# Attention in another order, slot sums copied in halves, and the last part's start resequenced

## Chip, core and metric

The kernel runs on one core of one Trainium2 chip. The metric is device microseconds (us) of one execution. TensorE (PE, with its weight loads PEld) multiplies, VectorE (DVE), ScalarE (ACT) and GpSimd (POOL) work elementwise, and SyncE (SP) issues most of the DMAs. Products go into PSUM, which has eight banks of 512 float32 columns; the other operands lie in SBUF.

## The reference

Three layers, one behind the other, all in float32: attention with pooled queries, a soft mixture of eight experts with four slots each, and a feed-forward layer with g = h cos h.

```python
q_pool = q.reshape(B, H, S // 2, 2, D).mean(axis=3)      # (4, 8, 576, 64)
attn = softmax(scale * q_pool @ k^T)                     # keys: 1152
x = (attn @ v) -> (2304, 512)
logits = x @ phi                                         # 32 slots
d = softmax(logits, over tokens); slot_in = d.T @ x
slot_out[e] = relu(slot_in[e] @ w1[e]) @ w2[e]
c = softmax(logits, over slots);  x2 = c @ slot_out
h = x2 @ w_in; g = h * cos(h); out = g @ w_out           # (512, 2048), (2048, 512)
```

## The kernel before

The kernel has two parts. The first holds attention and the mixture of experts. Its `attention()` only makes a list of 2,677 small operations, each a function with its dependencies; a string, `ORDER`, gives the sequence in which they are emitted (two characters of `DIGITS` are the number of one operation), and `in_order` walks it. So the order on every engine's queue is what `ORDER` says. An operation that needs a place takes the next free one: `"2"` are four places of two PSUM banks each, `"E"` five places in SBUF for exponentials, `"W"` twenty for expert weights. A place comes free when the last operation that uses its content has been emitted, and its next taker waits on the chip until that one is done.

Two heads are one pair `p`, 16 pairs in all; the queries of a pair are worked in two halves `a`, the 1152 keys in nine blocks `t`. For a pair, `sum_q` adds pooled neighbours (VectorE), `tr_q` and `tr_k` transpose (TensorE), `q_hi`, `k_hi` round to the fast format on ScalarE and `q_lo`, `k_lo` keep the rest on VectorE. `max_pair` multiplies rounded parts for a first maximum, `max_pair_red` reduces it on VectorE, `max_neg`, `max_row` and `max_put` turn it into a row. `scores(p,a,t)` is eight matmuls, `exps` the exponential on ScalarE, `av` the product with v, `av_out` its copy. `e_sum(p,a,t)` adds the exponentials up on GpSimd, or on VectorE where the digit t stands in `VEC[2*p+a]`. `load_v(p)` issues the DMA of v on SP's queue. Spread among this is `conv_*(i)`, which brings the last layer's weights to a rounded form for a fast product: loads, two passes on ScalarE, three on VectorE, `conv_round` on GpSimd, and `conv_store` back to DRAM on SP's queue.

At the end of the first part `o_mm` sums the slot outputs in one PSUM bank, `so_copy` (L1029) brings them to SBUF, `so_turn` (L1033) transposes and spreads them into four blocks of 128 columns, `so_put` (L1041) copies those to `soT`. `c_back(3)` and `c_keep(3)` do the same for the last token weights `cT`; in `ORDER` the sequence is so_copy, c_back(3), so_turn, so_put, c_keep(3).

The second part is emitted as the tuple `START` says, and then by a loop. `load_win_q` and `load_w` issue 1 MB DMAs of the converted weights. `p` (`p_some`, L1580) multiplies soT with 128 columns of w_in and keeps a rounded high part and a low part in `Pst`; `r` (`p_rows`, L1593) does it for 1,024 columns at once with 32 rows a piece, giving p_hi and p_lo, which `q` (`p_put`, L1609) spreads over Pst. A unit is one or two blocks of 128 columns of w_in for 256 tokens. `u` (`emit_u`, L1634) multiplies Pst and cT, ScalarE and VectorE bring the phase into range; `g` takes the sine and square on ScalarE, g, hi on VectorE and lo on GpSimd; `o` (`emit_o`, L1666) multiplies hi with w_hi and w_lo, and lo with w_hi. `s` (`split_w`, L1562) splits w_out's block f: a copy to w_hi by VectorE if `SPLIT[f]` is 2 or 3, otherwise by ScalarE, and the subtraction that leaves w_lo by GpSimd if it is odd, otherwise by VectorE. The first block of tokens has units of f = 0; 1; 2, 3; 4, 5; and so on. So o3 needs w of f = 4 and 5, o4 of 6 and 7, o8 of 14 and 15. The last unit's result is copied in halves by ScalarE and VectorE before its store (L1684).

Of the kernel before, what the change touches and what calls it, by code (L numbers as in the profile page):

```python
# [30 lines left out]
SPLIT = (0, 1, 1, 3, 1, 1, 1, 3, 2, 0, 1, 0, 3, 3, 0, 1)  # L31
# [23 lines left out]
    "1ZYJYL1O1S1P1T1X2V2W10112X1b1c2e2f1d4Q2c1W1a1e1g1h1k1l2d4SYM1o1i1s1p1tYN2k2lYKYO2-301f1j1m1n1r2Y1x2Z1y2i1q1u1v1w"  # L55
    "2g1-2j2hYQYP1z2031322324272o2p282m1+222n2q6T2t2u4V4W2xYR262AYS2y2B2r002s214Y4T25364U374X393D3AYTYU3E6W4Z4a3H3I4b"
    "296U3BYV2C3F3J3L2D2v2z383MYWYX2+2E3C3G3K3O3P2w4c4d3Q3R3U3V334g4h3Y3Z4e34354f3c2F4k3N3d2G4l3h3i3k4m4x3S3W3T4yYY2H"
    "2I3l3X4nYZYa3b3f3g4s4t3o3pYb3s3w3a3m3q4oYc4i3t3uYd3jYe3x3n3r3v3z4j3+4p3-Yg404q4r433eYf3y444u47484B55412J42454649"
    "4C2K56cAYh4A4E4F534R514v4w6X54526Y6b5A5D5B5H5LYjYk5E5FYl5P4-4D5I5J6Z5MYi5C5G5K5O8r506a6c5Q5S5N4z5TYo6d4+6e6fYmYn"
    "5U5V575Y5c5Z5d6u6v5g5h6k4G4H4I58595X6l5b5fYp6V5j5R5W8uAv5aYq73Yr5e5i5l5k5m745o5p8s5q5s5t6g5w5+Ys5x6h634JYt5-6q6r"  # L60
    "6i6j4K4L5n5r5vYuYv645u5y67686m6n6w6x5z61Yw714M62726B6F6C6G6o6s608x8yYx6p6t666A8v6y6z65696D8w6+8+6E8z6H6I6J4N8-90"
    "7E7H4O917F7I7J7L7P7MYzY+7Q6-7T707UcB6K6L92Y-Ay6M757776937G7KYy7O7S7W7XZ07896977N7R7V7Y7c7Z7g7d9E7h7k9F797A7b7f7B"
    "9A6N7l9I9J9BZ2Z17C7j7D7n7oZ3Z48t7p7a7e7q7s7t98Z56O6P7w7+7xAw7i99Z67u7y827-94959C9D6Q7r7v7zCz8180Z783858687889G8B"
    "ZA9H8C9K8F8G8J849NAz9L8K7mZ8Z9898D8H8A8E9O8I8M9McCA+B19TZB8N9c9d9U9f9gZD9j8L6R9k9P6S9QZCZE9n9o9h9l9r9pZF9sZG8O8P"
    "8QA-B3B09R9SZIcDB49e9i9mB2B59q9u9vBE9V9w9+BF9x9WZH9-8RA2A6A39X9YBA8S9t9y9zA7A1A59Z9aA0BB8T8U9bA9AAABAEA4A8D0ZJZK"
    "ACAFBGBHZLAIAJC+AMAQANZMAGB8ARBKAxZNZOBLADAHALB9APATAUBCBDAVAW8V8WAZAaAdAKAOB6ZQAhAeB7BIBJAi8X8YZP8ZBMBNASBVBWAY"
    "AcAgD1BOBPZRZTAkBQ8aAlD2D5ZSBgBhF1AXAbAfAjBjBnZUBkBZBlBoBaZVBrBvBsD3Bw8bBp8cD4BtB+ZYZWBTBiBUB-BmBqD6D7D8D9BXBYAm"
# [11 lines left out]
    "KSKMHMKTJPK8K9KEKWKbKXKfHNLkKQKUKJKNKRNhKVKZKcLlLmKYaZcNabKgKaKdKFKGHFHGHHHIcOacKjKhKkadagKnKoKsaaaeKvLxKeKiKmaf"  # L79
    "KtKwKxKlKpKqJQJRLyL-KrH9HAKzcPM0K+K-L1L2LrLsM1M2HOHQHPahL5LnJSajakNfHRLpaiL6alLoLqamKuJTKyL0L4L8L9LvLwLALzLBL+L3"  # L80
    "L7LELFLILJLtLuLMLNM3M6M7NkNlNnNiNjM4M5LCNmaoLDanaparLGLKLHLLLPLQMLMMMAMBMOMSMWMaasLOMPMQMTJUMXMEatQ3MbMNMRMVMUMZ"
    "MdMYMFMcMGJVM8aqawMeMfMjMHMgMnMkMrM9NtauMhMCMoMDavNuMiMlMmNgMIMqMsMuMvMpNoQ4NpNvMJMKNwNqaxLRLSayN-O0azMwMxMzN1Nr"
    "Q6MtM+N2N5N6N9NENsM-NAa+Nxa-O3LTN3N7b0MyNFO4N0NyN4N8NCNDNBNIO5NMNJNzO6b2NNNQN+O1NRLUO2O7cQQ9QAQCNGQDNHNLNPQELVLW"
# [1692 lines left out]
```

## Time and profile before

| | |
|---|---|
| runs | 731.6, 734.51, 735.19 us (median 734.51) |
| profiled execution | 732.33 us, span 730.5 us |
| TensorE busy | 717.4 us (98%) |
| VectorE, ScalarE, GpSimd busy | 569.7, 447.9, 407.2 us |
| attention and experts | to about 495 us of the span |
| head of the second part | 495 to 535 us |
| its steady part | 535 to 726 us |
| granted TensorE clock | 1.000 |

Busy time is the union of what the profiler shows of an engine's instructions. Matmuls overlap in the pipeline, so a short stop of TensorE is partly covered by the end of the matmul before it. A row of the timeline gives start, duration, engine, line, operation, and in brackets the idle time before it and what ended it.

### The profile page before, as it was taken

To read this page: it belongs to the slowest core of one execution; us is meant where nothing else is said; L and a number is where in the kernel's file an instruction comes from. 1 tells how busy PE (TensorE), PEld (TensorE's weight loads), DVE (VectorE), ACT (ScalarE), POOL (GpSimd) and SP (SyncE) were. 2 spreads that over 40 slices of the span, in tenths; PEclk is the share of its full clock that TensorE was granted. 3 is DMA by queue.
4 is the path that set the end of the run, shared out by engine and by line. 5 is a ranking of instruction groups with operands and counts; after the bars stand their busy time and mean duration, and the time that the engine had idled before them with its cause. 6 is when DMAs were issued, how large, how long until landed. Compare 5 with 4: busy or idle time off the path is not lost.

```text
span 730.5 us, 16465 instructions
## 1 busy us (share of the span) xinstructions
PE 717.4 (98%) x6428; PEld 530.7 (73%) x6428; DVE 569.7 (78%) x921; ACT 447.9 (61%) x846; POOL 407.2 (56%) x347
## 2 busy tenths in 40 slices
...
GB/s 221 145 98 157 173 134 130 209 162 141 191 130 187 199 156 160 182 191 102 171 102 147 183 163 259 360 410 414 11 30 30 0 30 30 30 9 20 31 29 30
DMA packets 75970, 101.48 MB, mean 139 GB/s; under 512 B 47156, under 2 KB 47540, under 8 KB 74996
## 3 DMA queue, kind: packets, MB, share of 16 engines
...
q14 instruction: 27, 0.22, 0.1%
...
## 4 chain that ended last, share of the span: by engine, by line
PE 89%; DVE 5%; DMA 2%; ACT 2%; issue 1%; POOL 0%; SPq 0%; DVEq 0%; ACTq 0%
PE mx L576 20%; PE o L1677 17%; PE mx L533 15%; PE o L1679 8%; PE mx L487 7%; PE mx L536 5%; PE u L1641 2%; PE mx L990 2%; PE mx L514 1%; PE mx L447 1%; PE mx L422 1%; DMA vn<-in_v_dram 1%; DMA w<-in_moe_w_dram 1%; PE mx L606 1%; DVE nm L496 1%; PE mx L384 1%
## 5 line engine op out<-in xcount | busy, mean ns | idle before, releaser
L565 POOL TENSOR_TENSOR ES<-ES,E 128x576 f32<-128x576 f32 (+2 forms) x149 | 215.5, 1447 | 93.0 <-DVE ES L565 54.9
L496 DVE TENSOR_REDUCE nm<-mx 128x2 f32<-128x768 f32 x240 | 220.8, 949 | 21.5 <-PE mx L487 20.3
L547 ACT ACTIVATE E<-mx 128x576 f32<-128x576 f32 (+2 forms) x288 | 175.1, 652 | 59.2 <-PE mx L536 42.3
L533 PE MATMUL mx<-Q,kX 64*128 64x288 f32 (+2 forms) x1152 | 163.8, 302 | 0.2 <-DVE avs L592 0.2
L576 PE MATMUL mx<-E,vn 128*64 128x288 f32 (+2 forms) x1152 | 157.8, 413 | 0.7 <-DMA vn<-in_v_dram 0.6
L1661 POOL TENSOR_TENSOR lo<-g,hi 128x512 fp32r<-128x512 f32 (+1 forms) x73 | 94.0, 1288 | 109.3 <-DVE hi L1659 103.1
L533 PEld LDWEIGHTS mx<-Q,kX 64*128 64x128 f32 x1152 | 109.6, 184 | 11.0 <-issue 2.6
L576 PEld LDWEIGHTS mx<-E,vn 128*64 128x64 f32 x1152 | 75.7, 136 | 57.0 <-ACT E L547 6.1
L1677 PE MATMUL o<-w_hi,hi 128*128 128x512 f32 x288 | 113.0, 392 | 0.6 <-DVE hi L1659 0.6
L1679 PE MATMUL o<-w_lo,hi 128*128 128x512 f32 x288 | 113.1, 393 | 0.3 <-DVE w_lo L1568 0.3
L533 PE MATMUL mx<-Q,kY 64*128 64x288 f32 (+2 forms) x576 | 87.4, 292 | 0.0
L536 PE MATMUL mx<-NM,one_row 64*128 64x288 f32 (+2 forms) x576 | 87.4, 291 | 0.0
L487 PE MATMUL mx<-kX,Q 64*128 64x384 f32 x490 | 84.7, 370 | 1.3 <-ACT Q L394 0.5
L1646 ACT ACTIVATE t<-u 128x512 f32<-128x512 f32 (+1 forms) x73 | 42.9, 591 | 58.6 <-PE u L1641 58.5
L1648 DVE SCALAR_TENSOR_TENSOR r<-t,u 128x512 f32<-128x512 f32 (+1 forms) x73 | 49.3, 678 | 36.3 <-ACT t L1646 35.7
L1677 PE MATMUL o<-w_hi,lo 128*128 128x512 f32 x288 | 77.3, 389 | 0.0
L1657 DVE SCALAR_TENSOR_TENSOR g<-r,u 128x512 f32<-128x512 f32 (+1 forms) x73 | 49.6, 679 | 35.2 <-ACT r L1655 34.4
L319 POOL TENSOR_TENSOR cvt<-cvt 128x512 uint32<-128x512 uint32 x32 | 40.9, 1279 | 46.4 <-ACT cvt L297 24.9
L487 PEld LDWEIGHTS mx<-kX,Q 64*128 64x128 f32 x490 | 44.1, 185 | 25.7 <-issue 10.9
L1677 PEld LDWEIGHTS o<-w_hi,lo 128*128 128x128 f32 x288 | 54.1, 188 | 11.3
L1677 PEld LDWEIGHTS o<-w_hi,hi 128*128 128x128 f32 x288 | 54.1, 188 | 10.8 <-DVE hi L1659 0.8
L1679 PEld LDWEIGHTS o<-w_lo,hi 128*128 128x128 f32 x288 | 54.2, 188 | 10.2 <-DVE w_lo L1568 0.6
...
## 6 DMA issues: line engine op xcount, KB each, us to landing
...
```

The costliest lines, as they stand in the source:

```text
L487: nc.tensor.matmul(out=m[:, h, 0:384], lhsT=Q1[p % 2][hs, AT[i]:AT[i] + 128], rhs=X[p][hs, ks], start=True, stop=True)
L496: nc.vector.tensor_reduce(out=nm3[p][:, i, :, c:c + 1], in_=m[:, :, 0:384], axis=AX.X, op=ALU.max)
L533: nc.tensor.matmul(out=sc[:, h, 0:n_q], lhsT=x[hs, ks], rhs=y[hs, qs], start=(n == 0), stop=False)
L536: nc.tensor.matmul(out=sc[:, h, 0:n_q], lhsT=one_row[hs, :], rhs=NM[p % 2][hs, qs], start=False, stop=True)
L547: nc.scalar.activation(out=e, in_=sc[:, :, 0:n_q], func=AF.Exp, scale=1.0 / 16.0)
L565: eng.tensor_tensor(out=ES[p, a], in0=ES[p, a], in1=E[p, a, t], op=ALU.add)
L576: nc.tensor.matmul(out=av_t[p, a, g][64 * h:64 * h + 64, 0:n_q], lhsT=vn[p][:, h, t, :], rhs=E[p, a, t][:, h, :], start=(t == g), stop=(t ...
L1648: nc.vector.scalar_tensor_tensor(out=r, in0=t, scalar=MAGIC, in1=u, op0=ALU.subtract, op1=ALU.subtract)
L1657: nc.vector.scalar_tensor_tensor(out=g, in0=r, scalar=1.0, in1=u, op0=ALU.subtract, op1=ALU.mult)
L1661: nc.gpsimd.tensor_tensor(out=lo[:, 0:n], in0=g, in1=hi[:, 0:n].bitcast(FP32), op=ALU.subtract)
L1677: nc.tensor.matmul(out=o, lhsT=x, rhs=w_hi[ff], start=(ff == 0 and not part), stop=bool(part and ff == NF - 1))
L1679: nc.tensor.matmul(out=o, lhsT=x, rhs=w_lo[ff], start=False, stop=False)
```

## The change

- `ORDER` is another sequence of the same operations in three stretches of attention: places 153 to 421 and 433 to 824 (about 32 to 76 and 76 to 153 us of the span) and 1494 to 1718 (269 to 309 us). Places 300 to 375, among them conv_store(3) at 323 and load_v(2) at 346, are the same.
- Seven strings of `VEC` differ; in all, VectorE has one `e_sum` fewer and GpSimd one more.
- `so_copy` copies in two halves on ScalarE, `so_turn` writes two PSUM banks instead of one, `so_put` copies the first half on ScalarE and the second on VectorE.
- The two `p` become one, `p_first`: both column blocks with the first half of the contraction, then both with the second. `r` for r = 0 is cut in three (quarter, quarter, half) with u0 and u1 between.
- Both `load_win_q` are issued ahead of both `load_w`.
- The splits come later, in the order of f; three copies and one subtraction go from VectorE to ScalarE and GpSimd. o2 is cut in two (8 products, then 4 by lo) with q(2,2), g4 and s6 between.
- The last result is copied by ScalarE alone.

```diff
-SPLIT = (0, 1, 1, 3, 1, 1, 1, 3, 2, 0, 1, 0, 3, 3, 0, 1)
+SPLIT = (0, 1, 1, 3, 1, 1, 1, 3, 1, 0, 1, 0, 1, 1, 0, 1)
 START = (
-    ("s", 1), ("p", 0, 0, 128), ("s", 2), ("p", 0, 128, 256), ("u", 0), ("s", 0), ("u", 1), ("g", 0),
-    ("r", 0), ("s", 3), ("g", 1), ("q", 0, 1), ("q", 1, 2), ("u", 2), ("o", 0), ("s", 5), ("s", 6), ("s", 4), ("u", 3),
-    ("g", 2), ("u", 4), ("o", 1), ("g", 3), ("r", 1), ("g", 4), ("s", 7), ("o", 2), ("q", 2, 2), ("s", 11), ("u", 5),
-    ("u", 6), ("s", 9), ("s", 10), ("q", 3, 2), ("s", 14), ("g", 5), ("o", 3), ("s", 8), ("s", 15), ("o", 4),
-    ("g", 6), ("s", 13), ("s", 12), ("u", 7), ("g", 7), ("u", 8), ("u", 9), ("o", 5), ("g", 8), ("u", 10),
+    ("p",), ("r", 0, 0, 1), ("u", 0), ("r", 0, 1, 2), ("u", 1), ("g", 0), ("r", 0, 2, 4), ("s", 0), ("q", 0, 1),
+    ("q", 1, 2), ("s", 1), ("g", 1), ("u", 2), ("o", 0), ("s", 2), ("s", 3), ("u", 3), ("u", 4), ("o", 1), ("s", 4),
+    ("g", 2), ("r", 1), ("s", 5), ("g", 3), ("o", 2, 0, 4), ("q", 2, 2), ("g", 4), ("s", 6), ("o", 2, 4, 8), ("s", 7),
+    ("u", 5), ("u", 6), ("s", 8), ("q", 3, 2), ("s", 9), ("g", 5), ("o", 3), ("s", 10), ("s", 11), ("o", 4),
+    ("g", 6), ("s", 12), ("s", 13), ("u", 7), ("g", 7), ("u", 8), ("u", 9), ("o", 5), ("s", 14), ("s", 15), ("g", 8), ("u", 10),
     ("g", 9), ("o", 6), ("u", 11), ("g", 10), ("o", 7), ("o", 8), ("o", 9),
 )
...
 VEC = (
-    "6", "1", "1268", "235", "1267", "26", "378", "13458",
-    "26", "18", "4", "38", "17", "56", "258", "1246",
-    "158", "3", "34567", "7", "125", "2", "36", "13456",
+    "6", "1", "178", "235", "1267", "27", "15", "1248",
+    "28", "138", "4", "38", "17", "56", "258", "1246",
+    "158", "3", "34567", "27", "125", "2", "36", "13456",
...
     def so_copy(i):
-        nc.scalar.activation(out=sh["so"], in_=sh["o"], func=AF.Copy)
+        for j in range(2):
+            cs = slice(j * DM // 2, (j + 1) * DM // 2)
+            nc.scalar.activation(out=sh["so"][:, cs], in_=sh["o"][:, cs], func=AF.Copy)
     def so_turn(i):
-        sh["s"] = mx()
+        sh["s"] = mx2()
...
-                out=sh["s"][:, kk * 128:(kk + 1) * 128], lhsT=sh["so"][:, kk * 128:(kk + 1) * 128],
+                out=sh["s"][:, kk // 2, kk % 2 * 128:(kk % 2 + 1) * 128], lhsT=sh["so"][:, kk * 128:(kk + 1) * 128],
...
     def so_put(i):
-        nc.vector.tensor_copy(out=sh["soT"].rearrange("p k s -> p (k s)"), in_=sh["s"])
+        for j in range(2):
+            o, x = sh["soT"][:, 2 * j:2 * j + 2].rearrange("p k s -> p (k s)"), sh["s"][:, j, 0:256]
+            if j:
+                nc.vector.tensor_copy(out=o, in_=x)
+            else:
+                nc.scalar.activation(out=o, in_=x, func=AF.Copy)
...
         for f in range(2):
             load_win_q(f)
+        for f in range(2):
             load_w(f, 2 - f)
...
-        def p_some(f, c0, c1, pm):
...
+        def p_first(pms):
+            for k0 in (0, 2):
+                for c, pm in enumerate(pms):
+                    cs = slice(128 * c, 128 * c + 128)
+                    for kk in range(k0, k0 + 2):
+                        nc.tensor.matmul(
+                            out=pm[:, 0:128], lhsT=soT[:, kk, :], rhs=win_q[0, kk][:, cs], start=(kk == 0), stop=(kk == HP - 1),
+                        )
+            for c, pm in enumerate(pms):
+                cs = slice(128 * c, 128 * c + 128)
+                nc.scalar.activation(out=Pst[0][:, cs], in_=pm[:, 0:128], func=AF.Copy, scale=INV2PI)
...
-        def p_rows(r, pm):
+        def p_rows(r, pm, k0=0, k1=HP):
             pm = pm[:, 0:256]
-            for kk in range(HP):
+            for kk in range(k0, k1):
...
+            if k1 < HP:
+                return
...
-                if last:
-                    h = DM // 2
-                    nc.scalar.activation(out=ob[:, 0:h], in_=o[:, 0:h], func=AF.Copy, scale=-TWOPI)
-                    nc.vector.tensor_scalar(out=ob[:, h:], in0=o[:, h:], scalar1=-TWOPI, scalar2=None, op0=ALU.mult)
-                else:
-                    nc.scalar.activation(out=ob, in_=o, func=AF.Copy, scale=-TWOPI)
+                nc.scalar.activation(out=ob, in_=o, func=AF.Copy, scale=-TWOPI)
...
-            for x in sorted(todo, key=lambda x: x[0]) if last else todo:
+            for x in (sorted(todo, key=lambda x: x[0]) if last else todo)[a:b]:
```

## Rows read from the trace of the kernel before

**Rows 1.** Windows: length, busy PE, PEld, DVE, ACT, POOL; clock, DMA share, GB/s

```profile
32.20:76.00 43.80, 42.58 (x454) 31.08 (x454) 42.56 (x60) 27.18 (x48) 28.87 (x22) 1.00 0.49 129
76.00:153.00 77.00, 77.00 (x889) 57.24 (x887) 71.83 (x110) 50.59 (x96) 51.78 (x41) 1.00 0.55 150
269.00:309.00 40.00, 40.00 (x439) 28.71 (x437) 36.60 (x54) 26.64 (x49) 26.60 (x21) 1.00 0.56 155
...
532.88:725.90 193.02, 192.99 (x902) 160.79 (x902) 115.01 (x192) 117.70 (x206) 84.48 (x65) 1.00 0.08 23
```

**Rows 2.** Timeline: the two matmuls that wait in the first stretch

```profile
48.16 0.45 PE L487 MATMUL mx<-kX,Q 64*128 64x384 f32 x2 [0.47 <-DVE kY L464]
...
74.23 1.16 PE L576 MATMUL mx<-E,vn 128*64 128x288 f32 x7 [0.65 <-DMA vn<-in_v_dram]
```

**Rows 3.** Waits of PE, 494 to 535 us: us in total, times, longest

```profile
PE pm L1583 <- DVE soT L1043: 0.8, 1, 0.8
PE u L1641 <- ACT Pst L1620: 0.7, 1, 0.7
PE pm L1614 <- ACT p_hi L1603: 0.6, 1, 0.6
PE o L1677 <- DVE hi L1659: 0.6, 2, 0.3
PE u L1641 <- DVE Pst L1589: 0.5, 1, 0.5
PE o L1679 <- DVE w_lo L1568: 0.3, 1, 0.3
PE u L1641 <- DVE g L1657: 0.2, 1, 0.2
```

**Rows 4.** Timeline: the first two products of o4

```profile
519.14 0.39 PE L1677 MATMUL o<-w_hi,hi 128*128 128x512 f32 x1
519.37 0.39 PE L1679 MATMUL o<-w_lo,hi 128*128 128x512 f32 x1
```

**Rows 5.** Groups by shape: running sums; busy us, mean ns, idle before

```profile
L565 POOL TENSOR_TENSOR ES<-ES,E 128x576 f32<-128x576 f32 x136 | 196.9, 1448 | 89.3 <-DVE ES L565 52.3 <-ACT E L547 10.2 <-DVE ES L563 7.7
L565 DVE TENSOR_TENSOR ES<-ES,E 128x576 f32<-128x576 f32 x73 | 55.6, 767 | 1.1 <-ACT E L547 0.2
```

**Rows 6.** Timeline: slot sums, from so_copy to the first product

```profile
495.84 0.60 ACT L1031 ACTIVATE so<-mx 128x512 f32<-128x512 f32 x1 [14.83 <-PE mx L1023]
...
496.49 1.16 PE L1036 MATMUL mx<-gsel,so 128*128 128x128 f32 x8
...
497.68 0.69 DVE L1043 COPY soT<-mx 128x512 f32<-128x512 f32 x1 [17.33 <-PE mx L1036]
...
498.43 2.05 PE L1583 MATMUL pm<-win_q,soT 128*128 128x128 f32 x16 [0.78 <-DVE soT L1043]
```

**Rows 7.** Timeline: the last result's two halves

```profile
725.95 0.38 ACT L1686 ACTIVATE ob<-o 128x256 f32<-128x256 f32 x1 [0.97 <-PE o L1677]
726.37 0.42 DVE L1687 TENSOR_SCALAR ob<-o 128x256 f32<-128x256 f32 x1 [0.93 <-ACT ob L1686]
```

**Rows 8.** Window of the first products, columns as in rows 1

```profile
498.43:503.42 4.99, 4.48 (x50) 3.16 (x50) 2.65 (x7) 2.98 (x8) 2.42 (x2) 1.00 1.01 422
```

**Rows 9.** Timeline: the row product and the first product of p_lo

```profile
501.49 1.93 PE L1599 MATMUL pm<-win_q,soT 128*32 128x256 f32 x32
...
504.41 0.39 PE L1615 MATMUL pm<-p_lo,spread 128*128 128x256 f32 x1
```

**Rows 10.** Timeline of POOL: a first split, a late one, a low half

```profile
498.31 1.26 POOL L1568 TENSOR_TENSOR w_lo<-w_lo,w_hi 128x512 fp32r<-128x512 f32 x1 [7.36 <-DMA w_lo<-w32o]
...
515.93 1.76 POOL L1568 TENSOR_TENSOR w_lo<-w_lo,w_hi 128x512 fp32r<-128x512 f32 x1
...
521.25 1.40 POOL L1661 TENSOR_TENSOR lo<-g,hi 128x512 fp32r<-128x512 f32 x1 [1.69 <-DVE hi L1659]
```

**Rows 11.** Groups by shape, POOL, 503 to 522 us: splits

```profile
L1568 POOL TENSOR_TENSOR w_lo<-w_lo,w_hi 128x512 fp32r<-128x512 f32 x6 | 8.3, 1396 | 0.8 <-ACT w_hi L1566 0.4 <-DVE w_hi L1564 0.4
```

More of the change, by code (lines that the diff above doesn't have):

```diff
@@ L54 @@
     "13151617191A1D1E0n1H0v1I2O2P0o0r2MYG142N182Q0w2R2S0s1B1F2T0l0m2U1C1G1K1L2a2b1MYH1Q1N0j1R0k1U0x1J1VYI1Y4P0t0y0u0-"
[L55 to L67, printed above, removed]
+    "1ZYJYL1O1S1P1T1X2V2W10112X1b1c2e2f1d4Q2c1W1a1e1g1h1k1l2d4SYM1o1i1s1p1tYN2k2lYKYO2-YQ1fYP1j1n1r302Y2Z1x1y2i1v1w2j"
@@ new lines @@
+    "2g2h1m1q1-203123322724281u2m2n1z212o2p2qYR1+222t2u4V2x2y262A2B4W2r4T4Y2s36393D4U4X6T373H3A3LYT3EYU253I6WYVYY292C"
+    "3M3B4Z2D2v2w2E3F2z2+4a336UYSYW383J3N3C3G3K3O344b3P35YX4g4h3Q3R4c4d3U3V3Y3Z4k4l3c3d4e4f3h3i3k3S3W2F2G4m4nYZYa4x4y"
+    "3T3X3b3f2H3l3m3a3g4s004tYb2I3o3s3w3p4o3qYc4i3t3uYd3jYe3x3n3r3v3z4j3+4p3-Yg404q4r433eYf3y444u47484B55412J42454649"
+    "4C2K56cAYh4A4E4F534R514v4w6X54526Y6b5A5D5B5H5LYjYk5E5FYl5P4-4D5I5J6Z5MYi5C5G5K8r6a6c5Q5O5N5S504z5TYo6d6e4+6fYmYn"
+    "5U5V575Y5c5Z5d6u6v5g5h6k6l4G4H4I58595X5bYpYq6V5R5W8u5f5jAv5a73Yr5e5i5l5k5m745o5p8s5s5t6g5w5+Ys5q636h4JYt5x5-6q6r"
@@ new lines @@
+    "6i4K5n5r6j5v5zYu6m644L4M6w5uYw5y60616n626x676o686p6B6C6F6G71726s6t8x8y8+6yYvYx8v658wYy8zcBYz696D666A6E6z6+6I6J8-"
+    "904N7E7H4O7L7F6H917P7T7I7M7Q7775Y+6K7U7G7K7O6L6MY-AyAw7J7N7679787A92Z0Z1937S7W7X6-707B7Y7Z7R7c967d977V7a7gZ27k9E"
+    "7e7h7i9A7b7f9F9B6N7j7l7n7o7C989IZ37D99Z47m7p7qCz9J7s7tZ57wZ6Z7ZA6O6P7u7x7+827y7-809C839D7r7v7z816Q85cC8694958788"
+    "9G9H8B9K8F8C848G8J8K9P9Q9T9UAz9L9M8A8E8I8MA+B1Z88NZ9898DZB9N9O9c9d9f9g8HZD8L9j9h8t9k9n9o6R9r6SZE9sZFZI9l9p8O8P8Q"
+    "A-B0B39tB49R9SZCZGB2ZH9e9i9m9qB59u9vBEBF9w9+9x9y9-9V9WA2A6A38R8S9X9Y9ZA7BG9zA18TA58U9a9bA0ZJA4A9BHAxD0AAABACBABB"
@@ L68 @@
+    "AEAFAIAJAMBKAQZLA8AGANAKB8B9BLZMZNADZKZOAHALAPARATAUBCBD8VAVcDAZAdAW8WAaAOASAeB6B7AhBIBJ8XZQAi8Y8ZZPZRZSBMBNBOAX"
+    "AbAf8aBVBWAYAcD1BPD2D5C+AgAkBQAlBgZTBhBjBnBkBZBrBvF1AjBoZUBaBsBwD38b8cZVBlBpD4B+BtZYZWBTBiBUB-BmBqD6D7D8D9BXBYAm"
     "BuAnAoByBxBz8d8eC-Bb8h8iC2C6C0BcBRC3CAC4F4C7C8CBZXZZZaBSDKBdDLC1C5C9CDCEcE8lCC8mcFBeBfHS8f8gDM8j8kDNCFCGCIZbZcCJ"
@@ L78 @@
     "J3J8JCJGJpJqLhLeLfLjLiH5H6J-HDKCKDHEJ9JDJHJLLcK0JKH7H8aRaTJMaUaVaSK1aWHJaXHKHLHBHCKAKHKBaYKKKIKLKOKPK4K2K5JNJOK3"
[L79 to L83, printed above, removed]
+    "KSKMHMKTJPK8K9KEKWKbKXKfHNLkKQKUKJKNKRNhKVKZKcLlLmKYaZcNabKgKaKdKFKGHFHGHHHIKjacKkNfKnKoKsKvLxcOKeaaKiKmKhKqadag"
+    "KtaeH9KlKpKwLyKxKrHAJQJRL-M0KzK+M1M2L1L5L2L6K-LrLsafahHOHQHPLpaiLnJSLvajHRakalJTKuKyaoL0L4LoLwL8L9amLqLALBLzL+LE"
+    "LFLILtLJLML3M6LuM3LNM7L7NkNlNnNiNjcPM4M5NmanaparLCLGLKLOLDLHLLLPLQNgaqMLMMMAMBMOMSMWMaMPasMTMQatMUMXMEJUMFMYauMN"
+    "MRMVMZMbMdJVMeMGawMfMHMgM8MjMnavMkM9MrNtMcMhMoNuMCMiMmMDMIMsMqMuMvNoQ3NvMJNpMKNwNqMlaxLRLSLTN-O0MwMxMzN1M+NrMpMt"
+    "azN2Q6N5N6NsN9NEa+M-N3N7NxO3NAayMya-N0N4O4N8NCNFNDNyO5O6NINJNMNNQ4Nzb2b0NBN+NQO1NRLUO2O7cQQ9QAQCNGQDNHNLNPQELVLW"
     "QFOCOEODO8LXO9NTb1NKNOS7NSOKOFb3b4OPNUOSOQb5OTOLOWOaOXOIObb6OeOJOGOHOfcRQ7ORQ8QBOVOZOALYb7QSOdOhOBLZNVOiNWOMONOO"
```

31 lines of the change are left out of this document (13 added, 18 removed).

## The prediction

> **What bounds the kernel now.** I read the busy shares by stage first, then the matmuls' waits, then the order of time where a wait stands. In the three stretches of attention whose order is rewritten TensorE is the bound: of 43.80 us it is busy 42.58, and in the other two for all of 77.00 and 40.00, at the full granted clock, while VectorE is busy 42.56, 71.83 and 36.60 [rows 1]. So a new order can win there only the 1.2 us in which no matmul runs. Two rows hold it: a max matmul at 48.16 waits 0.47 for VectorE's low half of k, a values product at 74.23 waits 0.65 for v [rows 2]. In the last part's head, 494 to 535, seven rows of waits add up to 3.7 us [rows 3]. A product of 512 columns is shown 0.39 long and is issued every 0.23 [rows 4], so a wait shown costs about 0.16 more than it says: eight waits, some 5 us in all. From there to the last product TensorE is busy 192.99 of 193.02 us [rows 1]. What can be won is thus some 1.5 us in attention, 5 in the head and a little at the end.
>
> **Attention.** The same operations are issued in another order, and seven strings of VEC differ, so that VectorE has one running sum fewer: 0.77 us off VectorE, 1.45 on GpSimd [rows 5]. Over the 161 us of the stretches that is nothing for either; it matters only where one of the two is late. The wait at 48.16 goes by the order: the matmul's PSUM bank came from k_lo(2,1) on VectorE, queued behind a conversion step and a sum of q; in the new order it comes from exps(1,0,4) on ScalarE, which has slack (27.18 busy of 43.80 [rows 1]). Worth 0.47 and the hidden 0.16: 0.6. The wait for v stays: load_v(2) keeps its place (346) in the order, behind the same conversion store on SP's queue, and a TensorE that comes earlier waits longer for it, unless the one VectorE sum less brings the conversion forward too. Count 0, bound 0.8. Against that, scores(1,0,3) now takes the bank of q_lo(2) with no TensorE work in between, where four other operations lay before; if VectorE is late there, it costs as much as a row of this kind, 0.5 to 0.8. Behind it are all the scores of that pair. Whether such places are worse in the other two stretches no row shows; their banks come as close before as after. I take 0.4 gained, with -1.2 (two new waits) and +1.5 as ends.
>
> **Slot sums.** Before: ScalarE copies so (495.84, 0.60), TensorE turns it (496.49, 1.16), VectorE copies soT (497.68, 0.69), and the first product starts at 498.43 [rows 6]. A half of 256 columns takes 0.38 on ScalarE and 0.42 on VectorE [rows 7]. After: the first half of so is there at 496.2, the turn can start about 496.3 (TensorE is at the weights' transposes until then), its first half is copied by ScalarE beside the turn of the second, and VectorE copies the second at 497.5. so_put stands ahead of c_keep(3) in ScalarE's queue, so the copy of cT, as large as so's (0.60 [rows 6]), is pushed behind it, to some 498.2; the first u needs it at 499.8, so this costs nothing, and would cost what it is late beyond 499.8 if that cover went. Then p starts at about 497.5: 0.9 earlier. Its second contraction half needs VectorE's half at 497.9 and comes to it at 498.4.
>
> **First rows and u.** Its sixteen matmuls took 2.05 with the drain of the last [rows 6]; the next can be issued from 499.4 on. The row product is cut in quarters and put between u0 and u1, so the wait of 0.5 for Pst [rows 3] is filled. It needs the second win_q block, moved ahead of w_lo on SP's queue; it lands some 2.5 us earlier than now, at 499.0 at the latest (1 MB at 422 GB/s [rows 8], counted back from the row product's start at 501.49 [rows 9]). The 32 row matmuls with u0 and u1 between them take 2.1, to 501.5, against 503.4 [rows 9]. p_hi now stands on ScalarE behind the sine and square of unit 0, p_lo on VectorE behind its g and hi; with four steps of 0.4 from u0's t, p_lo is there at 503.0, and its product follows at 503.05, against 504.41 [rows 9]: 1.4 kept. The wait for p_hi (0.6 [rows 3]) remains.
>
> **Splits.** The splits of f=1 and f=2 ran on GpSimd from 498.31 on, when it had nothing else [rows 10]. Now they stand behind the row product: ScalarE copies s0 after p_hi, then Pst's quarter, then s1, so GpSimd gets s1 at about 504.4. From there to w_lo7, which o4 needs, GpSimd has ten wide operations and a narrow one. Alone one takes 1.26, the worst took 1.76 [rows 10]; in the busy stretch the mean of a split is 1.40 [rows 11]. Ten at 1.40 and 0.75 is 14.7; and it idles about a microsecond before unit 4's low half, since that unit's sine waits on ScalarE for Pst2's copy, and that for q(2,2) behind the first eight products of o2. So w_lo7 is there at some 520.3 (519 to 521). After it o4 has seven of its twelve products left, 1.6 us: it ends at 521.9. Before it ran from 519.14 without a wait, twelve at 0.23, to 521.9 [rows 4]. The 1.4 us are spent at o4, to within 1 us. Then comes what VectorE is spared: the casts of f=8, 12 and 13 go to ScalarE and the subtraction of f=8 to GpSimd, 3 x 0.42 + 0.69 = 2 us by the nearest rows on VectorE [rows 6, 7]. Behind them stood the subtraction that o5 waits for (0.3), the g that frees u11's bank (0.2) and the hi that o8 waits for (half of 0.6) [rows 3]: 0.8 shown, 1.3 with what is hidden. GpSimd's seven wide operations from 520.3 to unit 7's low half take 9.8, to 530.1, which is just when o7 comes to it; s14 and s15 now stand ahead of g8, 1.2 us on ScalarE, which had waits to spare here. I take 1.2 for the whole head; ends -1 (GpSimd late by one more operation) and 3.6.
>
> A split on GpSimd took 1.26 at 498.31, in a quiet stretch, and 1.76 at 515.93, in a busy one [rows 10]. The Trainium skill (SBUF — State Buffer, Who interferes with whom) says that a VectorE instruction with two SBUF inputs and a GpSimd instruction that reads SBUF exclude each other, and the second waits for the first to end. By that rule every split moved from idle to busy time could pay what the 1.76 shows; by the mean of the rows it pays 0.14. The sum goes by the mean.
>
> **The last store.** Before, the two halves ran one after the other, ScalarE 725.95 and VectorE 726.37 to 726.79 [rows 7]. One copy of 512 columns is 0.60 [rows 6]: 726.55, 0.24 earlier, and nothing lies beside it.
>
> **Sum.** 0.4 + 1.2 + 0.24 = 1.8 us. The profiled execution took 732.33 with a span of 730.5; it would take 730.5. It lies 2.2 below the median of the runs, 734.51 (731.6 to 735.19), which becomes 732.7.
>
> **Rivals.** *All waits go:* GpSimd's operations cost 1.29 or less and its order leaves no gap, so that o4 keeps what the start won and the three later waits go too, 3.6; both waits of attention go, 1.2; with 0.24 that is 5.0 and 729.5. For it speaks that GpSimd idles for 1.69 until 521.25 before [rows 10]; against, that it must now do two splits more after 504. Chance 0.22. *Nothing is kept but the store:* the start's gain is spent at o4, the spared VectorE time is spent by s14, s15 and a late low half, and attention's new wait equals the one removed: 734.3. For it: what sets the end of a queue of eleven operations is its start, and that moves 6 us later. Chance 0.22. *Slower, by GpSimd and VectorE in each other's way:* at 1.76 for each wide operation w_lo7 comes at 523.0 and o4 ends at 524.6, and nine more to unit 8's low half end at 538.8, so that o8 ends 4.1 us later than now; less 0.24 and 0.4 that is 3.5 slower, 738.0. It decides from a mean of about 1.53 on; the mean of 1.40 before, with less crowding, is the evidence on both sides. At a mean of 1.65 it gives 736.3. Chance 0.10.
>
> **How the numbers follow.** The forecast, 732.7 (731 to 734), has 0.46. The range of 729.2 to 735.8 leaves out half of the first rival and more than half of the last. A measurement of this kernel can tell 0.5%, 3.7 us, from no change: faster means below 730.8, slower above 738.2. Faster: most of the first rival and the low edge of the forecast, 0.25. Slower: the top of the last and an attention with several new waits, 0.06. Within: 0.69.
>
> **What would show it.** Right: the first product of soT at 497.5 less what attention gained, relative to the last slot product; the row product ended 1.9 earlier; a wait of o4 for GpSimd's w_lo; no wait of o5, u11 and o8; 0.24 at the end; attention's rewritten stretches shorter by under 1 us. Wrong: a wide GpSimd operation in the head above 1.5 or below 1.3 on average; o4 without a wait; matmul waits of half a microsecond in attention that were not there.

## The result, and the profile after

The changed kernel takes 739.25 us (median of ten runs, 735.28 to 745.52), the kernel before 734.74 beside it (731.6 to 738.25). The ratio is 1.0071, 95% interval 1.0042 to 1.0100: slower by some 5 us, where 1.8 us faster were forecast, and with a spread of 10 us instead of 7. The profiled execution took 738.41 us with a span of 736.6, against 732.33 and 730.5.

| stretch of the profiled execution, us | before | after | difference | forecast |
|---|---|---|---|---|
| start to the first copy of the slot sums | 495.84 | 500.75 | +4.91 | -0.4 |
| from there to the end of the last product | 230.08 | 231.48 | +1.40 | -1.2 |
| from there to the end of the span | 4.6 | 4.4 | -0.2 | -0.24 |

The windows that answer to [rows 1] (length, busy PE, PEld, DVE, ACT, POOL; clock, DMA share, GB/s; the first two rewritten stretches, laid between the same scores as before, then the last part):

```profile
32.20:78.00 45.80, 42.91 (x456) 30.92 (x454) 41.83 (x60) 28.05 (x49) 30.68 (x23) 1.00 0.46 124
78.00:155.90 77.90, 77.61 (x887) 57.22 (x883) 71.21 (x109) 50.78 (x96) 52.88 (x40) 1.00 0.54 147
500.75:732.23 231.48, 226.35 (x1115) 185.56 (x1113) 141.93 (x232) 145.11 (x261) 111.65 (x85) 1.00 0.14 47
```

TensorE's work is what it was (42.6 and 42.9 us busy in the first stretch) at the same granted clock, 1.00. The first stretch is 2.0 us longer, and 1.7 of that is idle time of TensorE. The waits of PE from 30 to 535 us name it (total, times, longest); they answer to [rows 2, 3]:

```profile
PE o L1690 <- ACT r L1667: 1.6, 1, 1.6
PE o L1692 <- POOL w_lo L1575: 1.5, 2, 1.0
PE mx L533 <- ACT E L547: 1.5, 1, 1.5
PE pm L1593 <- ACT cT_r L1117: 1.1, 1, 1.1
PE mx L576 <- ACT part L818: 0.8, 1, 0.8
PE mx L576 <- DMA vn<-in_v_dram: 0.8, 1, 0.8
PE mx L514 <- DVE Z L502: 0.8, 2, 0.5
PE pm L1627 <- ACT p_hi L1616: 0.6, 1, 0.6
PE pm L1628 <- DVE p_lo L1617: 0.4, 1, 0.4
```

The wait for kY and those for soT, Pst, g and the later hi are gone. In their place stand ScalarE (E, r, cT_r) and GpSimd (w_lo). The wait for part is no mark of the new order: runs with the order of before in attention have it too (0.8 in e2, 0.4 in e13). That for VectorE's Z is a mark of it: it is 0.3 in the kernel before and 0.8 in each run with the new first stretch of which it was read (e1, e3, e5 and e12, beside this one).

**The wait of 1.5 us in the first stretch.** The timeline of SyncE, ScalarE and TensorE there:

```profile
50.20 0.33 SPq L285 DMA_DIRECT2D raw<-in_moe_w_in_dram  x1
50.63 0.61 SPq L340 DMA_DIRECT2D kn<-in_k_dram  x1
51.98 2.78 SPq L323 DMA_DIRECT2D w32p<-cvt  x1
...
54.82 1.40 ACT L547 ACTIVATE E<-mx 128x576 f32<-128x576 f32 x2 [0.21 <-PE mx L536]
...
59.04 0.66 ACT L292 ACTIVATE cvt<-raw 128x512 f32<-128x512 f32 x1 [2.72 <-DMA w32p<-cvt]
...
59.60 0.65 ACT L297 ACTIVATE cvt<-raw 128x512 uint32<-128x512 uint32 x1
60.15 1.18 ACT L547 ACTIVATE E<-mx 128x576 f32<-128x576 f32 x2
60.84 0.40 PE L533 MATMUL mx<-Q,kX 64*128 64x288 f32 x2 [1.46 <-ACT E L547]
```

Read it from the bottom: the scores at 60.84 wait for exps that empty their PSUM bank. The exps run at 60.15, because ScalarE takes its instructions in order and ahead of them stands a conversion step (L292, L297). That step waits 2.72, since its only buffer cvt is still read by the store of the weights converted before, issued at 51.98 behind 1 MB of other loads. In the order before, one exp stood ahead of the step, which waited 0.74, and no matmul waited there:

```profile
57.09 0.65 ACT L547 ACTIVATE E<-mx 128x576 f32<-128x576 f32 x1 [0.89 <-PE mx L576]
58.48 0.69 ACT L292 ACTIVATE cvt<-raw 128x512 f32<-128x512 f32 x1 [0.74 <-DMA raw<-in_moe_w_in_dram]
```

**The slot sums**, which answer to [rows 6]:

```profile
500.75 0.66 ACT L1033 ACTIVATE so<-mx 128x256 f32<-128x256 f32 x2 [14.77 <-PE mx L1023]
...
501.32 1.16 PE L1038 MATMUL mx<-gsel,so 128*128 128x128 f32 x8
502.52 0.38 ACT L1050 ACTIVATE soT<-mx 128x256 f32<-128x256 f32 x1 [1.11 <-PE mx L1038]
502.80 0.59 ACT L1114 ACTIVATE cT<-mx 128x512 fp32r<-128x512 f32 x1
502.93 0.42 DVE L1048 COPY soT<-mx 128x256 f32<-128x256 f32 x1 [17.61 <-ACT soT L1050]
503.27 0.23 ACT L1117 ACTIVATE cT_r<-mx 128x64 fp32r<-128x64 f32 x1
503.56 0.49 PE L1593 MATMUL pm<-win_q,soT 128*128 128x128 f32 x2 [1.08 <-ACT cT_r L1117]
```

The two halves lie beside nothing. ScalarE's half starts when all eight turning products are done (501.32 + 1.16 = 502.48), VectorE's when ScalarE's is done. The first product waits for cT_r, which c_keep(3) copies behind so_put's half. It comes 2.81 after the first copy; before it came 2.59 after it.

**o2**, which waited 0.3 before and had no place in the forecast:

```profile
513.42 3.95 POOL L1575 TENSOR_TENSOR w_lo<-w_lo,w_hi 128x512 fp32r<-128x512 f32 x3
...
513.72 0.63 ACT L1573 ACTIVATE w_hi<-w_lo 128x512 fp32r<-128x512 f32 x1
...
514.24 0.63 ACT L1667 ACTIVATE r<-r 128x512 f32<-128x512 f32 x1
...
514.90 0.63 ACT L1668 ACTIVATE r<-r 128x512 f32<-128x512 f32 x1
515.56 0.69 DVE L1670 SCALAR_TENSOR_TENSOR g<-r,u 128x512 f32<-128x512 f32 x1 [0.62 <-ACT r L1668]
516.29 1.37 DVE L1672 CAST hi<-g 128x512 fp32r<-128x512 f32 x1
...
517.80 0.47 PE L1690 MATMUL o<-w_hi,hi 128*128 128x512 f32 x1 [1.57 <-ACT r L1667]
```

ScalarE casts a weight block (513.72) ahead of unit 2's sine (514.24). VectorE's cast to hi takes 1.37; it ends at 517.66, 0.29 after GpSimd's run of splits (513.42 + 3.95). The same cast where GpSimd is idle takes 0.43, later in this execution:

```profile
523.01 0.43 DVE L1672 CAST hi<-g 128x512 fp32r<-128x512 f32 x1
```

The wait of o2's product is put down to ScalarE's r, but that was done at 515.53: what came last is the cast.

The last store, which answers to [rows 7], is one copy as forecast:

```profile
732.26 0.60 ACT L1697 ACTIVATE ob<-o 128x512 f32<-128x512 f32 x1 [0.76 <-PE o L1690]
```

### The profile page after: what moved, and what is told of

Read it like the earlier page. It is cut to its first block, busy times and chain, and to the rows that moved or that the text cites. A ratio compares the mean times of both kernels' runs of the same rounds, so it can differ in the third digit from the quotient of the medians.

```text
span 736.6 us, 16470 instructions
## 1 busy us (share of the span) xinstructions
PE 719.2 (98%) x6428; PEld 531.0 (72%) x6428; DVE 568.4 (77%) x914; ACT 450.9 (61%) x851; POOL 411.8 (56%) x349
## 4 chain that ended last, share of the span: by engine, by line
PE 84%; DVE 6%; DMA 4%; POOL 2%; issue 2%; ACT 2%; SPq 0%; ACTq 0%; POOLq 0%; DVEq 0%
PE o L1690 17%; PE mx L576 17%; PE mx L533 13%; PE o L1692 9%; PE mx L487 6%; PE mx L536 4%; PE u L1654 2%; DVE nm L496 2%; PE mx L990 2%; DMA vn<-in_v_dram 1%; PE mx L514 1%; PE mx L447 1%; DMA w<-in_moe_w_dram 1%; PE mx L384 1%; PE mx L422 1%
## 5 line engine op out<-in xcount | busy, mean ns | idle before, releaser
L565 POOL TENSOR_TENSOR ES<-ES,E 128x576 f32<-128x576 f32 (+2 forms) x151 | 218.5, 1447 | 96.4 <-DVE ES L565 60.4
L1661 DVE SCALAR_TENSOR_TENSOR r<-t,u 128x512 f32<-128x512 f32 (+1 forms) x73 | 49.3, 678 | 35.8 <-ACT t L1659 35.3
```

Of the source, the lines that this page charges most:

```text
L565: eng.tensor_tensor(out=ES[p, a], in0=ES[p, a], in1=E[p, a, t], op=ALU.add)
L1661: nc.vector.scalar_tensor_tensor(out=r, in0=t, scalar=MAGIC, in1=u, op0=ALU.subtract, op1=ALU.subtract)
```

## The experiments

The theory: ScalarE's order is the cause. In attention a conversion step that waits for a transfer now stands ahead of exps; in the head casts stand ahead of unit 2's sine and of cT's copy. The rivals: PSUM banks that VectorE must free, the transfers alone, and interplay of the two parts. All ratios are to the kernel before. Steps of ORDER are given by name.

**e1 and e2: each part alone.**

```diff
 e1, the kernel before:
-ORDER, VEC of before
+ORDER, VEC of the changed kernel
 e2, the changed kernel:
-ORDER, VEC of the changed kernel
+ORDER, VEC of before
```

> The kernel before with the changed kernel's ORDER and VEC, and nothing of the head's edits. In the changed kernel's profile the first copy of the slot sums starts 4.9 us later than before (500.75 against 495.84), and from it to the last product it takes 1.4 us more. Theory (attention carries it by itself): first copy at 500 to 501.5, from there on as before, the time 4 to 6 us above the kernel before, ratio 1.005 to 1.008. Rival (the two parts act only together, or the loss is a disturbance of the profiled execution): first copy below 498 and a ratio below 1.003.

> The changed kernel with ORDER and VEC of the kernel before, so only the head and the last store are changed. Theory (the head loses by itself): from the first copy of the slot sums to the last product 231.5 us against 230.1, the end of the span 0.2 earlier after the last product, the time 1 to 1.5 us above the kernel before, ratio 1.0015. Rival (the head gains as forecast, and lost it only because the new attention order hands it busier queues): 228.9 us, ratio 0.998.

e1: ratio 1.0045 (1.0026 to 1.0064), 737.02 us; first copy of the slot sums at 500.65, from there to the last product 230.12. e2: 1.0026 (1.0003 to 1.0049); 230.87 for that stretch, and 0.26 saved behind the last product. Both parts lose by themselves, and 0.45% and 0.26% make up the 0.71%. But e2's first copy came at 498.73, 2.9 us later than in the kernel before, though its attention is the same instruction for instruction: one profiled execution cannot size a loss of 3 us in attention. The same holds for the +4.91 of the table above: 0.3 of it comes ahead of the rewritten places, and 1.5 behind 225 us, where runs with the order of before are up to 4.7 later too. From here on sizes in attention are ratios of many runs, and a profile says only which wait there is; e12 is followed by a table of what the profiles have in common. The head is different: over the ten profiles that have the old head, the stretch is 230.06 to 230.12.

**e3, e4, e5: the first stretch.**

```diff
 e3, the kernel before: places 153 to 299 and pair 1's VEC from the changed kernel
 e4, e3 with
-conv_sign(2), conv_load(3), e_sum(0,1,8) ... max_put(1,1), conv_store(2)
+conv_sign(2), e_sum(0,1,8) ... max_put(1,1), conv_store(2), conv_load(3)
 e5, e3 with
-conv_act(3), conv_low(3) ... exps(1,1,1) ... conv_clamp(3)
+... exps(1,1,1) ... conv_act(3), conv_low(3), conv_clamp(3)
```

> The kernel before with the changed order in the first rewritten stretch alone (places 153 to 299, and the running sums of pair 1's first half that go with it). Theory: it holds about 1.8 us of the loss: scores(1,1,8) starts 1.6 to 2.1 later than before, with a max matmul at about 60.8 waiting some 1.5 for ScalarE, whose conversion step waits 2.7 for the landing of the last conversion store; the first copy of the slot sums 1.5 to 2.5 later. Rival (the loss needs the later stretches too, being slack that is used up slowly): scores(1,1,8) less than 0.6 later.

> The kernel e3_stretch1 with one step moved: the load of the next weights to be converted, conv_load(3), goes from place 221 to behind conv_store(2), so that load_k(3) stands ahead of it in SyncE's queue again. Theory (ScalarE's conversion step waits for a transfer, which queues behind k and the new load): load_k(3) is issued near 46 instead of 50.6, the conversion step's wait of 2.7 falls to 1.2 or less, the max matmul's wait of 1.5 at 60.8 to 0.3 or less, and scores(1,1,8) starts less than 0.7 later than before. Rival (TensorE waits because VectorE has to free PSUM banks that now follow one another closely): the wait and the 1.8 us stay.

> The kernel e3_stretch1 with conv_act(3) and conv_low(3) moved in the order from place 276 to just ahead of conv_clamp(3), so that exps(1,1,1) stands ahead of them on ScalarE; the loads and stores stay as in e3. Theory (the exps stand behind a conversion step that waits for a transfer): the step still waits for the landing or comes to it later, but the scores no longer wait for ScalarE near 59 to 61 (wait under 0.2), and the time is 1 to 3 us below e3_stretch1, ratio to the kernel before 1.001 to 1.004. Rival (transfers themselves or PSUM banks hold TensorE, not ScalarE's queue): ratio as e3's 1.0057, and the wait near 59 to 61 stays.

e3: 1.0057 (1.0030 to 1.0085): by the time, of five runs, the stretch holds attention's loss. Its profile misses what was expected and meets the rival's condition: scores(1,1,8) starts under 0.6 later, exps from 78.6 to 225 us even 0.1 earlier than before, and the 3.4 by which the slot sums come later arises behind that, where the order is that of before. The same instructions were issued at the same times as in the changed kernel (the store at 51.77), but the store landed in time for the step to start at 57.47 after a wait of 1.37, and the scores waited 0.3 by starts. The landing alone moved by over a microsecond between executions whose order is the same up to there. e4: 1.0016 (0.9999 to 1.0033); k is issued at 46.91, the step still waits 1.43, now for its load. e5: 1.0024 (1.0006 to 1.0042), no wait of TensorE for ScalarE near 60. Each move takes back over half of e3's loss by the ratios; the intervals of e3 and e5 still touch, and neither of the moved steps uses a PSUM bank, as the rival would want.

**e6, e13, e14: single steps put into the order before.**

```diff
 e6, the kernel before:
-load_k(3) ... conv_sign(2) ... conv_store(2) ... conv_load(3)
+conv_sign(2), conv_load(3), load_k(3) ... conv_store(2)
 e13, the kernel before:
-exps(1,1,1) ... conv_act(3), conv_low(3)
+conv_act(3), conv_low(3), exps(1,1,1)
 e14: both
```

> The kernel before with one step changed: conv_load(3) goes from place 278 to behind conv_sign(2), and load_k(3) right behind it, as the two stand in the new order. Theory (this step alone makes the new wait): load_k(3) is issued near 50 instead of 45.5, the conversion store lands after 58.5 instead of 56.4, ScalarE's conversion step waits 1.5 to 2.5 instead of 0.74, a max matmul near 61 waits 0.5 to 1.5 for ScalarE, and the time is 1 to 3 us above the kernel before, ratio 1.0015 to 1.004. Rival (the load's place matters only together with the other moves of the stretch): ratio 1.000 and no wait.

> The kernel before with conv_act(3) and conv_low(3) moved from places 284 and 285 to ahead of exps(1,1,1), which the new order also does; all loads and stores stay. Theory (a conversion step that waits for its transfer matters as soon as exps stand behind it): the step waits 1 to 2 for its load (before: 0.74 with an exp ahead of it), a scores matmul near 60 waits 0.3 to 1.0 for ScalarE, ratio 1.0005 to 1.002. Rival (the rest of the rewritten order is needed): ratio 1.000 and no new wait of TensorE.

> The kernel before with both steps: conv_act(3) and conv_low(3) ahead of exps(1,1,1), and conv_load(3) and load_k(3) right behind conv_sign(2), ahead of the conversion's store on SyncE's queue. Theory (the two together make the loss of the first stretch): the step waits 1.5 to 2.7 for the store's landing, a scores matmul near 61 waits 0.8 to 1.6 for ScalarE, ratio 1.002 to 1.005. Rival (the rest of the rewritten order is needed): ratio below 1.0015.

e6: 0.9997 (0.9979 to 1.0016), no wait of TensorE for ScalarE near 60, as its rival has it. The place of the load alone is not seen to cost anything. e13, where one conversion step passes one exp: 1.0029 (1.0006 to 1.0052), 2.1 us (0.4 to 3.8), above the 1.002 expected at most; in its profile the stretch is 1.1 longer. Its timeline:

```profile
57.40 0.67 ACT L292 ACTIVATE cvt<-raw 128x512 f32<-128x512 f32 x1 [1.85 <-DMA raw<-in_moe_w_in_dram]
...
59.21 0.40 PE L533 MATMUL mx<-Q,kX 64*128 64x288 f32 x2 [0.99 <-ACT E L547]
```

e14: 0.9997 (0.9976 to 1.0018). Against the theory, and as its rival has it, the two steps together don't add up: with the load ahead, the step waits 0.84 and the scores 0.2, since it starts at 57.25 against 57.40 in an execution whose scores run 0.9 later. The reading is that the exp behind the step is what costs, that how much depends on how late the last of the step's transfers lands, and that the place of a load can help or hurt. In e14 it helps, in e4 the opposite move helped. A rule on loads can't be drawn from this.

**e7 and e9: the other two stretches.**

```diff
 e7, the kernel before: places 375 to 824 and 1494 to 1718 and their VEC from the changed kernel
 e9, e7 with
-conv_act(7), max_put(3,1), conv_low(7) ... exps(3,1,0), exps(3,1,1), conv_clamp(7)
+max_put(3,1) ... exps(3,1,0), exps(3,1,1), conv_act(7), conv_low(7), conv_clamp(7)
```

> The kernel before with the changed order and running sums in the second and third rewritten stretch alone (places 375 to 824 and 1494 to 1718). Theory: they hold the smaller part of attention's loss, 0.8 to 1.7 us by the changed kernel's profile (0.9 in the second stretch, about 0.8 at 283), ratio 1.001 to 1.0025, with a conversion step that waits over 2 for its load near 112. Rival (all the loss is made in the first stretch and only carried on): ratio 0.999 to 1.0005.

> The kernel e7_stretches_2_3 with conv_act(7) and conv_low(7) moved from places 576 and 579 to just ahead of conv_clamp(7), behind the row maxima's copy and two exps on ScalarE. Theory (ScalarE's queue stands behind a conversion step that waits for its load): the matmul on NM at 111 no longer waits (1.0 by starts), the second stretch loses at least 0.8 less than the 2.3 us of e7's profile, the time falls by 0.7 to 1.5 us, ratio to the kernel before 1.000 to 1.002. Rival (the loss of these stretches is spread over many banks and VectorE): the ratio stays at 1.0028 and new waits for VectorE show near 112.

e7: 1.0028 (1.0004 to 1.0053). Here, too, a conversion step stands ahead of a row maximum's copy (NM) and of exps:

```profile
103.72 0.37 SPq L285 DMA_DIRECT2D raw<-in_moe_w_in_dram  x1
...
110.23 0.66 ACT L292 ACTIVATE cvt<-raw 128x512 f32<-128x512 f32 x1 [2.98 <-DMA raw<-in_moe_w_in_dram]
110.79 0.31 ACT L521 ACTIVATE NM<-mx 128x192 fp32r<-128x192 f32 x1
...
111.16 0.40 PE L536 MATMUL mx<-NM,one_row 64*128 64x288 f32 x2 [0.94 <-ACT NM L521]
```

e9: 1.0004 (0.9982 to 1.0026), the same place with the step moved back:

```profile
109.19 0.33 ACT L521 ACTIVATE NM<-mx 128x192 fp32r<-128x192 f32 x1 [2.05 <-PE mx L514]
110.34 1.20 ACT L547 ACTIVATE E<-mx 128x576 f32<-128x576 f32 x2 [0.82 <-PE mx L536]
111.42 0.66 ACT L292 ACTIVATE cvt<-raw 128x512 f32<-128x512 f32 x1
```

The step finds its load landed, and a smaller wait of 0.7 for E comes two microseconds later. In this pair of profiles the second stretch loses 0.9 less (1.4 against 2.3 by the scores at both ends), but that is one pair, the intervals of the two ratios overlap, and the table behind e12 does not bear it out: that the step's place makes the second stretch's loss is not shown.

**e8, e10, e11: the head.** e8 and e11 have the order of before in attention.

```diff
 e8, e2 with
-("s", 4), ("g", 2), ("r", 1),
+("g", 2), ("s", 4), ("r", 1),
 e11, e8 with
-("g", 3), ("o", 2, 0, 4), ("q", 2, 2), ("g", 4), ("s", 6), ("o", 2, 4, 8), ("s", 7),
+("g", 3), ("s", 6), ("o", 2, 0, 4), ("q", 2, 2), ("s", 7), ("g", 4), ("o", 2, 4, 8),
 e10, the changed kernel with
-so_turn(0), so_put(0), c_keep(3)
+so_turn(0), c_keep(3), so_put(0)
```

> The kernel e2_head_only with one pair of START swapped: the sine, square and gate of unit 2 ahead of the split of the fifth weight block. Theory (o2 waits 1.7 because ScalarE does two casts more ahead of its sine, and because VectorE's cast to hi is held while GpSimd's run of splits lasts, 1.37 instead of 0.6 to 0.7): that cast takes under 0.9, o2's wait falls to 0.8 or less, and the stretch from the slot sums' first copy to the last product falls from 230.87 to 229.8 to 230.3. Rival (o2 waits for something both orders share, or o4 takes the gain back): o2's wait over 1.3, or 230.7 or more for the stretch.

> The changed kernel with c_keep(3) put ahead of so_put(0), so that ScalarE copies cT and cT_r while TensorE turns the slot sums. Theory (the first product waits for cT_r's copy, which frees its PSUM bank): the first product comes 2.2 us after the first copy of the slot sums instead of 2.81, and its wait is for soT; the stretch from there to the last product falls from 231.47 to 230.8 to 231.0. Rival (the wait moves on, since o2's and o4's waits set the head's end): the first product 2.2 and the stretch still 231.3 or more. In the time it is within the spread either way.

> The kernel e8_head_g2_first with the splits of the seventh and eighth weight blocks moved ahead in START, to behind the gate of unit 3 and to ahead of the gate of unit 4. Theory (o4's two waits, 1.25 and 0.67 by starts, are for GpSimd's subtractions, which stand behind the low half of unit 4 that is needed 1.9 us later): both w_lo are there in time, o4 waits 0.5 or less in all, and the stretch from the slot sums to the last product falls from 229.75 to 228.2 to 228.8; the time 2 us below the kernel before, ratio 0.996 to 0.998. Rival (GpSimd's queue as a whole is late): the wait moves to o5, u7 or o6, and the stretch stays at 229.4 or more.

e8: 0.9985 (0.9962 to 1.0007), the stretch 229.75 against e2's 230.87. One swap is worth 1.1 us, and it does two things that were not taken apart: counted from the first copy, the gate g of unit 2 comes 0.5 earlier, with less ahead of its sine on ScalarE, and its cast, with two splits on GpSimd ahead of its end instead of three, is 0.7 shorter:

```profile
510.34 2.72 POOL L1575 TENSOR_TENSOR w_lo<-w_lo,w_hi 128x512 fp32r<-128x512 f32 x2
...
512.68 0.67 DVE L1672 CAST hi<-g 128x512 fp32r<-128x512 f32 x1
...
513.49 0.47 PE L1690 MATMUL o<-w_hi,hi 128*128 128x512 f32 x1 [0.34 <-DVE hi L1672]
...
514.73 2.55 POOL L1575 TENSOR_TENSOR w_lo<-w_lo,w_hi 128x512 fp32r<-128x512 f32 x2
...
516.06 1.50 DVE L1672 CAST hi<-g 128x512 fp32r<-128x512 f32 x1
...
522.00 0.50 PE L1692 MATMUL o<-w_lo,hi 128*128 128x512 f32 x1 [1.09 <-POOL w_lo L1575]
```

Unit 2's cast begins 0.38 before the two splits end at 513.06 and takes 0.67, to 0.29 after them; unit 3's, which now meets the two splits of 514.73 to 517.28, takes 1.50, to 0.28 after them. o4's wait stays. e11: 0.9980 (0.9959 to 1.0001); o4's waits for w_lo are gone, but the stretch is 229.49, only 0.26 better:

```profile
521.99 1.20 PE L1690 MATMUL o<-w_hi,lo 128*128 128x512 f32 x4 [0.72 <-POOL lo L1674]
532.30 1.20 PE L1690 MATMUL o<-w_hi,lo 128*128 128x512 f32 x4 [0.62 <-POOL lo L1674]
```

The rival holds: GpSimd's queue is late as a whole, and what stands last in it is waited for. e10: the first product 2.21 after the first copy, the stretch 230.85 against 231.48, as expected; it waits for soT now. Its ratio, 1.0035 (1.0014 to 1.0055), is lower than the 0.6 us explain; it was taken beside other runs of the kernel before than the 1.0071, and it shows how far two medians of an attention of this kind lie apart.

**e12: the changed kernel with the four moves** (conv_act and conv_low of 3 and 7 behind the exps, c_keep(3) ahead of so_put(0), the gate of unit 2 ahead of the fifth split).

> The changed kernel with four moves: conv_act(3) and conv_low(3), and conv_act(7) and conv_low(7), behind the exps as in the runs above; c_keep(3) ahead of so_put(0); the gate of unit 2 ahead of the fifth split. Theory (ScalarE's queue, in attention behind transfers and in the head behind casts, holds nearly all of the loss): ratio to the kernel before 1.000 to 1.003, against 1.0071, and the stretch from the slot sums to the last product 229.6 to 230.0. Rival (these are symptoms, and the order as a whole runs TensorE into other waits): ratio 1.005 or more.

1.0006 (0.9988 to 1.0024), not told from the kernel before, and 229.75 for the head. Against the changed kernel's 1.0071 (1.0042 to 1.0100) six steps moved by some places take back nearly all of the loss, but the 1.0071 was taken beside other runs. Beside the same runs of the kernel before stands e10, which has one of the four moves: 1.0035. The other three take back some 2.1 us from there, 1.1 of them in the head (230.85 to 229.75), so about 1 us in attention. Versions better than both kernels are e8 and e11, by 1 to 1.5 us, which their intervals don't quite tell from nothing.

**What the profiles have in common.** How much longer than in the kernel before a stretch of attention took, in us, by the starts of the same exps (at 35.5, 72.1 and 225.3 in the kernel before) and the first copy of the slot sums:

| order in the stretch | first stretch | second stretch | from there to the slot sums |
|---|---|---|---|
| of before | -0.1 to 0.1 (e2, e7, e8, e9, e11) | -0.5 to 0.6 (nine profiles) | 0.1 to 4.7 (nine profiles) |
| changed, conversion step ahead of exps | 0.4 to 1.5 (after, e1, e3, e4, e10) | 0.6 to 2.2 (after, e1, e7, e10) | |
| changed, step put back behind them | -0.1, 0.0 (e5, e12) | 1.5, 1.1 (e9, e12) | |
| changed, no such step moved | | | -0.2 to 3.3 (six profiles) |
| of before, step put ahead (e13), load too (e14) | 1.1, 0.2 | | |

In the first stretch the loss goes with the step's place, about 1 us. In the second there is a loss with the step in either place, so its cause is open. Behind 225 us profiles differ most where nothing was changed.

## Why the prediction was wrong, point by point

**Attention: forecast 0.4 gained, measured 3.3 us lost (e1).** The failed step is "I take 0.4 gained, with -1.2 (two new waits) and +1.5 as ends". The working looked at PSUM banks that VectorE frees and at one load of v on SyncE's queue; ScalarE was counted as slack (27.18 busy of 43.80 [rows 1]). The moves of conv_act, conv_low, conv_load and conv_store went uncosted. Slack of an engine says nothing about what stands behind a waiting instruction in its queue. The trace of before had the row to see it: the conversion step at 58.48 waits 0.74 for its load with an exp safely ahead of it. What the runs showed in place of the two new PSUM waits is a step with a known wait, put ahead of exps that TensorE needs: 2.1 us by itself in e13's runs (0.4 to 3.8), 1.1 in its profile, and about 1 us of the first stretch over the profiles. The rest of the 3.3 lies in the second stretch, 0.6 to 2.2 in four profiles, and its cause stays open; part of it, or of the first, can be VectorE's Z (0.3 to 0.8), which the working held to be nothing. The feared wait of scores(1,0,3) did not come; that for kY went and that for v stayed (0.65, then 0.8), as forecast.

**Slot sums: forecast 0.9, measured 0.4 gained (e2: 2.20 against 2.59) or 0.2 lost (after).** Two assumptions failed: that a half of soT can be copied while the other half is turned, and that VectorE's half runs beside ScalarE's. And "this costs nothing" for cT's copy was wrong in the changed kernel: the cover named was the first u, but the first product already waits for cT_r. In e2, with another ORDER, the same copy is not waited for.

**p_lo: forecast 1.4, measured 0.2 (8.37 after the first copy in e2, 8.57 before) or 0.4 later (8.98, after).** From unit 0's t to p_lo there are seven steps, not four: t at 503.91 in e2, p_lo done at 507.05, 3.1 us. The wait for p_hi stayed, 0.6, as forecast; one of 0.4 for p_lo came behind it.

**o2: no term, 1.7 us.** START's new order was followed on GpSimd's and VectorE's queues, but not on ScalarE's between unit 2's t and its sine; nor was the cast to hi priced beside a split. The Trainium skill (SBUF — State Buffer, Who interferes with whom) was drawn on for VectorE's instructions with two SBUF inputs alone; the same section names cast and copy among those that can take the pair of ports shared with GpSimd, when they run in a mode that uses two ports, and says that whoever issues first has the pair for the whole instruction, while the other is blocked. The rows agree in that the cast ends with GpSimd's work: 1.37 and 1.50 where splits ran on beside it, both ending 0.3 after them, and 0.43 with GpSimd idle. The trace of before has such a cast as well (0.73 at 510.39, to 0.29 after a split).

**o4, o5, u11, o8: right in the main.** o4 waits for GpSimd's low halves, 1.4 forecast and 1.8 by starts measured; but the larger part, 1.1, is for the block before w_lo7, which the working took to be there. The three later waits are gone. A split has a mean of 1.39 in the head, as forecast, so the rival with GpSimd at 1.53 or more is not what made the kernel slower:

```profile
L1575 POOL TENSOR_TENSOR w_lo<-w_lo,w_hi 128x512 fp32r<-128x512 f32 x8 | 11.0, 1394 | 0.3 <-ACT w_hi L1573 0.3
```

**The last store: right**, 0.2 of 0.24.

The head's sum let the start's gain be spent at o4, so that o4 would end level with the kernel before, counted from the first copy, and then took 1.2 as gained. Measured, o4 ends 2.9 later: o2 is 1.7 behind, the wait for Pst that is gone wins 0.8 of that back, and o4 adds 2 us that no gain of the start was there to pay. The three later waits then bring 1.5 back, more than the 1.2 forecast, which leaves the +1.4. The range's end of 3.6 for *all waits go* is 0.9 more than the two terms named for it, 1.4 and 1.3. The larger error is attention's. By time the head's loss is 1.9 us (e2), with an interval that reaches down to the 0.5 of its profile. The chance of 0.06 for slower was too small because attention's bound counted waits of one kind.

What stays open: the cause of the second stretch's loss; which of the other moves of the first stretch, VectorE's Z among them, make up the rest of e3's loss beyond e5 by the time; and what sets how late a transfer lands.
